# Attention and two MoE layers on one core: the first four attention tiles from plain query rows, with whole-tile exponentials

## The chip, the cores and the metric

The kernel runs on 1 core of one Trainium2 chip. The metric is the time of one execution in device microseconds (us); the time of a version is the median of several runs.

## What is computed

Chunked attention, then a leaky-ReLU layer pair, then a Mish layer pair, all in fp32 accuracy (the weights arrive as fp64 words and are converted on the chip).

```python
# attention: q, k, v of 4 batches x 8 heads x 768 positions x 64, 8 memory rows per head; chunk of 32 queries
for c in range(nc):                       # 24 chunks; left context 16, right context 8
    k_full = concat(mem_k, k[l_start:r_end])
    scores = scale * q_c @ k_full.T       # scale = 1/8
    scores = scores - max(scores)
    a = exp(scores)
    a = a / (sum(a) + 1e-09)
    out[c] = a @ concat(mem_v, v[l_start:r_end])
x = out as 3072 rows x 512
h = x @ w_in;  g = max(h, 0) + alpha * min(h, 0);  x = g @ w_out      # 512 -> 2048 -> 512
h = x @ w2_in; g = h * tanh(softplus(h));          y = g @ w2_out     # 512 -> 2048 -> 512
```

## The kernel before

The 3072 tokens are cut into 24 attention tiles T of 128 tokens and into 6 blocks of 512 tokens; block 0 takes the tiles T = 0 to 3 (`T0` = 4). For a block, `gemm1` (L1210) multiplies the block with a 128-column slice j of W_in (j = 0 to 15), `act1` (L1229, L1230 on ScalarE, L1233 on VectorE) applies the leaky ReLU, `split_g` (L1222, L1223) splits the result into a high and a low fp32r part, and `gemm2` (L1259) adds it into four PSUM banks. Each fp32 product is three fp32r products (high x high, high x low, low x high).

No engine order is written by hand. `Plan` collects tasks with an engine, a cost and a due time, and `Plan.run` schedules them: an engine takes the ready task with the earliest due time, and the due times come from the TensorE program, which is a list in order. The order of the instructions of each engine is then fixed. While TensorE would stand idle in the plan before the first `gemm2`, `Plan.run` fills in matmuls of a zero tile (`busy`, L1758).

The opening, up to the first `gemm1`, is this. For T = 0 to 3, `load_qk` loads the keys (`kw`, L626) and the query rows (L635), and `place` copies the rows (L277, on VectorE, for T = 0 also on ScalarE) into a tile `qbd` in which the two heads of a pair stand block-diagonal, with zeros written by GpSimd (L584). `scores_of` then computes 16 products of 128 x 64 x 64 per tile (L738) into a bank. `rest` of `scores_of` does the softmax: the row maximum (`top`, L753), for T = 0 and 1 a scaling of the maximum (L783) and eight exponentials of 64 columns each with their row sums (`exps`, L756, ScalarE); for T = 2 and 3 (`WHOLE`) one subtraction on VectorE (`less`, L763), one exponential of the whole tile (L766) and one row sum (`total`, L769); then 1e-9 is added (L786), the reciprocal taken (L787) and the tile multiplied (`norm`, L772). `turn_pe` transposes in two halves (L974), and `copy_on` (L277) takes each to the tile `aT`; `values_of` multiplies with the values (L805) and writes x as a high part (L822, ScalarE) and a low part (L826, VectorE). The scores lie in `s_bufs` and the transposes in `a_bufs`, two tiles of each, so T = 2 and 3 reuse the tiles of T = 0 and 1. The steps run in the order

```python
first = "s0 s1 t0 s2 t1 s3 v0 t2 v1 t3 v2 v3"
```

The weights come in through `load_raw` (L340 for W_in, L345 for W_out, 512 KB each), and `to_f32` turns the fp64 words into fp32: `scale` (L365, ScalarE), `high` (L368) and `low` (L371) on VectorE for the first eight; `split_w` makes the fp32r parts (L404 ScalarE, L407 VectorE). All loads stand in one queue, SP's. A `gate` (L608) is a DMA of one element out of a loaded tile: SP waits there until that tile has landed (or been scaled), and what stands behind it in the queue is issued only then. The first two columns of W_in are multiplied in two halves of the block's tokens, so that tokens of T = 0 and 1 don't wait for T = 2 and 3:

```python
for half in range(2):
    for j in range(SPLIT):          # SPLIT = 2
        gemm1(0, 0, j, xts[0], BN, half)
```

From T = 4 on other functions do the attention (`load_qk_late` L651, L658, L666; `scores_late` L861; `turn_late` L998; `values_late` L927), in pairs of tiles between the products of the blocks. They load into `kt` and into the same `qbd` tiles.

Of the kernel before, what the change touches and what calls it, by code (L numbers as in the profile page):

```python
# [200 lines left out]
def chunked_attention_moe_moe_kernel(  # L201
# [39 lines left out]
    WHOLE = (2, 3)  # L241
# [77 lines left out]
    PLAIN = 8  # L319
# [11 lines left out]

    def load_raw(item, **kw_):
        layer, side, j = item
        w = {(0, "i"): w1_in, (0, "o"): w1_out, (1, "i"): w2_in, (1, "o"): w2_out}[layer, side]
# [17 lines left out]
    def to_f32(item, raw, **kw_):  # L352
        late = bool(behind_wide)
        f = wfs.next()

        def words():
            t = raw.t if item[0] == 0 else raw.t.bitcast(U32).rearrange("p (f w) -> p f w", w=2)
            return t[:, :, 0], t[:, :, 1]
# [8 lines left out]
        def high():  # L367
            nc.vector.tensor_scalar(f.t, words()[1], 3, None, ALU.logical_shift_left)  # L368

        def low():  # L370
            nc.vector.scalar_tensor_tensor(f.t, words()[0], 29, f.t, ALU.logical_shift_right, ALU.bitwise_or)  # L371

        def three():
            t = raw.t.bitcast(U16)
            t = t if item[0] == 0 else t.rearrange("p (f w) -> p f w", w=4)
            nc.scalar.activation(words()[0], t[:, :, 1], AF.Identity, bias=floors, scale=2.0**-13)
# [7 lines left out]
        def both():  # L384
            nc.vector.scalar_tensor_tensor(f.t, words()[1], 3, words()[0], ALU.logical_shift_left, ALU.bitwise_or)

        if late:
            add("act", a_(512), negative, [raw], [f], **kw_)
        add("act", a_(512), scale, writes=[raw], **kw_)
        if item in w1_items[:2]:  # L390
            gate(raw, 0.0, lambda: words()[1][0:1, 0:1].bitcast(F32))
        if item in w1_items[:PLAIN]:
            add("dve", d_(512, True), high, [raw], [f])
            add("dve", d_(512), low, [raw], [f])
        else:
            add("act", a_(512), three, writes=[raw], **kw_)
            if late:
                add("dve", d_(512), with_negative, [f], [raw])
            add("dve", d_(512), both, [raw], [f])
# [161 lines left out]
    qbd = [own([P, 1024], f"qbd{i}") for i in range(2)] + [spare_slot() for _ in range(2, T0)]  # L561
# [9 lines left out]
    s_bufs = [own([P, 1024], "s"), spare_slot()]  # L571
    a_bufs = [own([P, 1024], "aT"), spare_slot()]
# [4 lines left out]
    for b in s_bufs:  # L577
        for cols in (slice(0, CH), slice(CH + SW, P)):
            add("pool", 0.6, lambda b=b, cols=cols: nc.gpsimd.memset(wide_of(b)[:, :, cols], 0.0), writes=[b])
    for b in qbd:  # L580
        for h in range(2):
            add(
                "pool", 0.6,
                lambda b=b, h=h: nc.gpsimd.memset(  # L584
                    b.t.rearrange("p (g h x) -> p g h x", g=2 * NP, h=2)[(1 - h) * 64 : (2 - h) * 64, :, h], 0.0
                ),
                writes=[(b, 2 + h)],
            )
    stats = ring(ac, [P, 3, 2 * NP], F32, "st", 3)
# [5 lines left out]
    n_ps = [0]  # L595

    def att_bank(T, late):
        n_ps[0] += 1
        return bank((0, 1, 2, 4, 5, 6, 7)[n_ps[0] % 7] if T < T0 else late)

    gated = dp.tile([1, 16], F32, name="gated")
    n_gates = [0]

    def gate(b, when, first=None):
        n = n_gates[0]
        n_gates[0] += 1
        add(
            "sp", 0.001, lambda: nc.sync.dma_start(gated[:, n : n + 1], first() if first else b.t[0:1, 0:1]), [b],  # L608
            at=-1.0, not_before=when,
        )  # L610

    def load_qk(T):
# [5 lines left out]
        qt = qbd[T]  # L618
# [4 lines left out]
        def qview():  # L623
            return qt.t.rearrange("p (a e h x) -> p a e h x", a=NP, e=2, h=2)

        add("sp", dma_(P * NP * KC * 4), lambda: nc.sync.dma_start(kview(), kw[b, t]), writes=[kt])  # L626
        if T == 3:
            gate(kt, 12.7)

        row = q_rows[T // 2], T % 2  # L630

# [3 lines left out]
        add("sp", dma_(P * 2048), lambda: nc.sync.dma_start(rows(), q[b, t].rearrange("h d a e x -> (h d) (a e x)")), writes=[row])  # L635
        for h in range(2):

            def place(eng, h=h):
                half = slice(h * 64, (h + 1) * 64)
                copy_on(eng, qview()[half, :, :, h], rows()[half].rearrange("p (a e x) -> p a e x", a=NP, e=2))  # L640
# [35 lines left out]
    def load_v(T):  # L676
        b, t = divmod(T, TPB)
        if T < T0:
# [3 lines left out]
            add("sp", dma_(P * 3520), lambda: nc.sync.dma_start(view(), src), writes=[v])  # L682
            if T in (0, 2):
                gate(v, 14.7 if T == 0 else 0.0)
# [31 lines left out]
    def scores_of(T):  # L716

        t = T % TPB
        (kt, kview), (qt, qview) = kts[T], qs[T]
        bk = att_bank(T, 6)  # L720
        sb = s_bufs[T % 2 if T < T0 else 0]

# [23 lines left out]
        def clip():  # L746
            if t == 0:
                nc.vector.memset(ps()[0:64, 0:NP, 0:16], NEG)
# [1211 lines left out]
```

## Time and profile before

| | |
|---|---|
| median of 3 runs | 1034.07 us (1033.57 to 1034.28) |
| profiled execution | 1034.0 us, its span 1032.1 us |
| TensorE busy | 1020.7 us, 99% of the span |
| granted TensorE clock, mean | 0.998 |
| VectorE, ScalarE, GpSimd busy | 834.1, 641.8, 6.9 us |
| first `gemm1` product starts | 23.59 us |
| third column of W_in (j = 2) starts | 30.47 us |

The execution's own time is 1.9 us over its span. A busy TensorE is the union of modelled intervals, so busy does not mean that every slot is used. Times below count from the span's start.

### The profile page before, as it was taken

The page shows a single profiled execution, that of the slowest core. Times are in us where ns is not written, and L with a number is a line of the kernel's source. Part 1 is how long each engine was busy: PE and PEld are TensorE (multiplying, and loading weights), DVE is VectorE, ACT ScalarE, POOL GpSimd, SP SyncE. Part 2 cuts the span into 40 slices and gives each one's busy share as a digit, 9 for nine tenths or more (in the row PEclk, how much of TensorE's full clock was granted, in tenths as well). Part 3 has the DMA queues.
Part 4 walks back from the last instruction along what each step waited for, and adds up shares of the span by engine and source line. Part 5 has one row for each costly group of instructions (what it writes and reads, how often), then busy time and mean ns, then how long its engine had stood idle before and what let it go on. Part 6 is the DMA issues. An engine that isn't in the chain of part 4 may idle for free.

```text
span 1032.1 us, 19612 instructions
## 1 busy us (share of the span) xinstructions
PE 1020.7 (99%) x7195; PEld 842.1 (82%) x7197; DVE 834.1 (81%) x1481; ACT 641.8 (62%) x1401; POOL 6.9 (1%) x20
## 2 busy tenths in 40 slices
PE   8999999999999999999999999999999999999997
PEld 6888888888888788888888888888888888888886
DVE  7877688888878889999999969697578777578784
ACT  6899756656665655797977657564444744444630
POOL 2000000000000000000000000000000000000000
PEclk9999999999999999999999999999999999999999
DMA  8977785875687773734878899886778766668766
GB/s 254 318 249 241 245 286 168 258 252 177 223 265 268 243 243 123 255 113 165 296 243 292 296 319 322 306 259 193 227 233 261 218 194 193 192 193 262 209 193 146
DMA packets 133929, 242.35 MB, mean 235 GB/s; under 512 B 12874, under 2 KB 50250, under 8 KB 133834
## 3 DMA queue, kind: packets, MB, share of 16 engines
q1 hardware_dynamic: 131658, 240.05, 73.6%
q10 hardware_dynamic: 2176, 1.05, 0.5%
q8 instruction: 57, 0.93, 0.4%
q14 instruction: 38, 0.31, 0.1%
HBM read 182.33 MB, written 58.72 MB: 234 GB/s over the span
## 4 chain that ended last, share of the span: by engine, by line
PE 97%; DMA 1%; ACT 0%; SPq 0%; issue 0%; DVE 0%; ACTq 0%
PE bank L1522 29%; PE bank L1364 22%; PE bank L1259 17%; PE bank L1210 17%; PE bank L1701 7%; PE bank L927 2%; PE bank L861 1%; DMA wo<-in_w_out_dram 1%; PE bank L1494 1%; DMA wo<-in_kw_dram 1%; PE bank L1758 0%; PE bank L805 0%; PE bank L738 0%; PE bank L998 0%; SPq L635 0%
## 5 line engine op out<-in xcount | busy, mean ns | idle before, releaser
L1210 PE MATMUL bank<-xh,wi 128*128 128x512 f32 (+1 forms) x528 | 170.1, 385 | 0.9 <-ACT rstrip L1230 0.9
L1259 PE MATMUL bank<-gh,wo 128*128 128x512 f32 x512 | 170.3, 392 | 0.2 <-issue 0.2
L1210 PEld LDWEIGHTS bank<-xh,wi 128*128 128x128 f32 x528 | 98.2, 188 | 20.7 <-ACT rstrip L1230 1.1
L1259 PEld LDWEIGHTS bank<-gh,wo 128*128 128x128 f32 x512 | 96.0, 188 | 20.6
L1364 PE MATMUL bank<-wo,wo 128*128 128x512 f32 x438 | 111.1, 389 | 0.0
L1210 PE MATMUL bank<-xl,wi 128*128 128x512 f32 (+1 forms) x264 | 101.1, 383 | 0.0
L1259 PE MATMUL bank<-gl,wo 128*128 128x512 f32 x256 | 99.7, 390 | 0.0
L1364 PEld LDWEIGHTS bank<-wo,wo 128*128 128x128 f32 x438 | 82.2, 188 | 17.0
L1522 PE MATMUL bank<-wi,wo 128*128 128x512 f32 x294 | 73.6, 389 | 0.0
L1229 ACT ACTIVATE rstrip<-bank 128x512 f32<-128x512 f32 x64 | 40.7, 636 | 50.7 <-PE bank L1210 50.4
L1364 PE MATMUL bank<-wo,wi 128*128 128x512 f32 x282 | 71.2, 389 | 0.0
L1522 PEld LDWEIGHTS bank<-wi,wo 128*128 128x128 f32 x294 | 55.2, 188 | 11.4
L1522 PE MATMUL bank<-wi,wi 128*128 128x512 f32 x258 | 64.5, 389 | 0.0
L1222 ACT CAST gh<-rstrip 128x512 fp32r<-128x512 f32 x64 | 42.5, 663 | 35.4 <-PE bank L1259 20.4
L1233 DVE SCALAR_TENSOR_TENSOR rstrip<-rstrip,nalpha 128x512 f32<-128x512 f32 x64 | 47.9, 749 | 19.6 <-ACT rstrip L1230 19.1
L1364 PEld LDWEIGHTS bank<-wo,wi 128*128 128x128 f32 x282 | 52.9, 188 | 11.0
L1223 DVE TENSOR_TENSOR gl<-rstrip,gh 128x512 fp32r<-128x512 f32 x64 | 44.2, 690 | 19.6 <-ACT gh L1222 18.8
L1522 PE MATMUL bank<-gh,wo 128*128 128x512 f32 x228 | 58.0, 389 | 0.0
L1015 DVE STREAM_TRANSPOSE aT<-s 32x256 f32<-32x256 f32 x128 | 55.7, 435 | 2.5
L1210 PEld LDWEIGHTS bank<-xl,wi 128*128 128x128 f32 x264 | 49.6, 188 | 9.4
L1522 PEld LDWEIGHTS bank<-wi,wi 128*128 128x128 f32 x258 | 48.4, 188 | 10.0
L1259 PEld LDWEIGHTS bank<-gl,wo 128*128 128x128 f32 x256 | 48.1, 188 | 10.1 <-issue 0.5
(354 smaller groups left out, 2181.7 us busy)
## 6 DMA issues: line engine op xcount, KB each, us to landing
wo<-w2i SPq DMA_DIRECT2D x102, 256.0 KB, 3.0
wo<-w2o SPq DMA_DIRECT2D x100, 256.0 KB, 3.7
wi<-w2o SPq DMA_DIRECT2D x68, 256.0 KB, 3.3
wi<-w2i SPq DMA_DIRECT2D x66, 256.0 KB, 3.1
wo<-in_w_out_dram SPq DMA_DIRECT2D x24, 512.0 KB, 6.8
w2i<-wo SPq DMA_DIRECT2D x24, 512.0 KB, 3.2
w2o<-wo SPq DMA_DIRECT2D x24, 512.0 KB, 3.2
wo<-w1o SPq DMA_DIRECT2D x22, 512.0 KB, 4.8
```

Of the source, the lines that this page charges most:

```text
L861: nc.tensor.matmul(ps(z)[row : row + CH, i, 2 * a + e, :], qview()[half, 2 * a + z, e].rearrange("p (x c) -> p x c", c=2)[:, :, c], keys(2 ...
L927: nc.tensor.matmul(out[h * 64 : (h + 1) * 64, i, p, c], value(half, c, 2 * p + h), aT()[half, i, (p % 2) * (NP // 2) + p // 2, c, h ^ (p % ...
L1015: nc.vector.transpose(dst[:, :, m // 2, m % 2], src[:, :, keys])
L1210: nc.tensor.matmul(bk.t[:, lo:hi], a, b, start=kk == 0 and i == 0, stop=kk == KT - 1 and i == 2)
L1222: add("act", a_(n), lambda: nc.scalar.copy(g.t[0], src.t[0]), [src], [(g, "h")], at=at)
L1223: add("dve", d_(n), lambda: nc.vector.tensor_sub(g.t[1], src.t[0], g.t[0].bitcast(F32)), [src, (g, "h")], [(g, "l")], at=at)
L1229: add("act", a_(n) - 0.05, lambda: nc.scalar.activation(m.t[0], h.t[:, :n], AF.Relu, scale=-1.0), [h], [m], at=at)
L1233: lambda: nc.vector.scalar_tensor_tensor(r.t[0], m.t[0], nalpha[:, j : j + 1], r.t[0], ALU.mult, ALU.add),
L1259: nc.tensor.matmul(bk.t[:, :n], lt, rh, start=j == 0 and i == 0, stop=j == NJ - 1 and i == 2)
L1364: nc.tensor.matmul(bk.t, l, r, start=start and kk == n == 0, stop=kk == 1 and n == 2, skip_group_check=True,)
L1522: nc.tensor.matmul(bs[db].t, l, r, start=first and k == 0, stop=p == pairs[-1] and k == 2, skip_group_check=True,)
L1701: nc.tensor.matmul(bk.t, l, r, start=start and kk == n == 0, stop=kk == 1 and n == 2, skip_group_check=True,)
```

## The change

Only the opening changes.

- Scores: the block-diagonal copies and their zeros go. The query rows are the stationary operand directly, 32 products of 64 x 32 x 64 per tile (two heads times two 32-query chunks, in different halves of rows and columns of the array).
- Softmax: all four tiles take whole-tile exponentials. For T = 0 and 1 VectorE subtracts the maximum (`less_here`); for T = 2 and 3 (`ON_PE`) TensorE adds the negated maximum to the scores' bank by one fp32 product of the identity with the broadcast maxima (`less`), and ScalarE reads the bank. The 1e-9 is now in two padding columns of the score tile, written once by GpSimd, and the row sum takes them in.
- Rooms: each of the four tiles has its own score tile (two of them the `qbd` tiles) and its own `aT` tile; banks are set by a table (`EARLY`).
- Order: the four scores first, then `t0 t1 v0 v1 t2 t3 v2 v3`.
- Loads: no gates; the first loads have fixed places in the queue; the first two columns of W_in come in one load of 1 MB (`load_first`), into the `xh1` tile, which block 1 uses later.

```diff
-    WHOLE = (2, 3)
+    ON_PE = (2,3,)
+    FIRST, PLAIN = 0, 8
+    def load_first():
+        raw = Buf(xmakers[1][0])
+        xring.last[1] = [raw]
+
+        def go():
+            to = raw.t.bitcast(U32).rearrange("p (k f) -> p k f", k=KT)
+            nc.sync.dma_start(to, w1_in[:, : 2 * P].bitcast(U32).rearrange("(k p) f -> p k f", p=P))
+
+        first_load(P * 8192, go, raw)
+        first_raw.append(raw)
...
+        if first_raw and item in w1_items[:2]:
+            return first_raw[0]
...
-        if item in w1_items[:2]:
-            gate(raw, 0.0, lambda: words()[1][0:1, 0:1].bitcast(F32))
...
-    qbd = [own([P, 1024], f"qbd{i}") for i in range(2)] + [spare_slot() for _ in range(2, T0)]
+    qbd = [own([P, 1024], f"qbd{i}") for i in range(2)]
...
-    s_bufs = [own([P, 1024], "s"), spare_slot()]
-    a_bufs = [own([P, 1024], "aT"), spare_slot()]
+    s_bufs = [own([P, 1024], "s"), spare_slot(), *qbd]
+    a_bufs = [own([P, 1024], "aT"), *(spare_slot() for _ in range(1, T0))]
...
+        for rows, col in ((slice(0, 64), CH - 1), (slice(64, P), CH + SW)):
+            add("pool", 0.1, lambda b=b, r=rows, c=col: nc.gpsimd.memset(wide_of(b)[r, :, c : c + 1], 1e-9), writes=[b])
...
+    EARLY = {"s": ((4,), (5,), (0,), (1,)), "t": ((6, 7), (2, 4), (7, 0), (1, 2)), "v": ((5,), (6,), (7,), (0,))}
...
+    def first_load(size, go, buf):
+        n_first[0] += 1
+        add("sp", size / 330e3, go, writes=[buf], at=n_first[0] - 100.0)
...
-            add(BOTH if T == 0 else "dve", 0.55, place if T == 0 else partial(place, "dve"), [row], [(qt, h)])
-        kts[T], qs[T] = (kt, kview), (qt, qview)
+        first_load(P * 2048, lambda: nc.sync.dma_start(rows(), q[b, t].rearrange("h d a e x -> (h d) (a e x)")), row)
+        first_load(P * NP * KC * 4, lambda: nc.sync.dma_start(kview(), kw[b, t]), kt)
+        kts[T], qs[T] = (kt, kview), (row, qview)
...
-                        nc.tensor.matmul(
-                            ps()[c * 64 : (c + 1) * 64, e * NP + p, :],
-                            qview()[:, p, e].rearrange("p h (x c) -> p (h x) c", c=2)[:, :, c],
-                            kview()[:, p, k0 : k0 + SW],
-                            start=True, stop=True,
-                        )
+                        for h in range(2):
+                            half, lo = slice(h * 64, (h + 1) * 64), c * 64 + h * CH
+                            nc.tensor.matmul(
+                                ps()[lo : lo + CH, e * NP + p, :],
+                                qview()[half, p, e].rearrange("p (x c) -> p x c", c=2)[:, :, c],
+                                kview()[half, p, k0 : k0 + SW],
+                                start=e == p == 0, stop=True, skip_group_check=True,
+                            )
...
         def less():
+            nc.tensor.matmul(
+                bk.t, ident, st.t[:, 0, :].unsqueeze(2).broadcast_to([P, 2 * NP, SW]), start=False, stop=True,
+                skip_group_check=True,
+            )
+
+        def less_here():
             nc.vector.tensor_add(s(), ps(), st.t[:, 0, :].unsqueeze(2).broadcast_to([P, 2 * NP, SW]))
 
         def exp():
-            nc.scalar.activation(s(), s(), AF.Exp, scale=0.125)
+            nc.scalar.activation(s(), ps() if T in ON_PE else s(), AF.Exp, scale=0.125)
...
-            if T in WHOLE:
-                add("dve", d_(512), less, [(st, 0), bk], [sb])
-                add("act", a_(512), exp, [], [sb])
-                add("dve", d_(512), total, [sb], [(st, 1)])
+            if T in ON_PE:
+                add("pe", 0.95, less, [(st, 0)], [bk])
             else:
-                add("dve", 0.12, lambda: nc.vector.tensor_scalar_mul(st.t[:, 0, :], st.t[:, 0, :], 0.125), [], [(st, 0)])
-                for g in range(2 * NP):
-                    add("act", 0.29, lambda g=g: exps(g), [(st, 0), bk], [(sb, g), (st, 1, g)])
-            add("dve", 0.12, lambda: nc.vector.tensor_scalar_add(st.t[:, 2, :], st.t[:, 1, :], 1e-9), [(st, 1)], [(st, 2)])
-            add("dve", 0.14, lambda: nc.vector.reciprocal(st.t[:, 2, :], st.t[:, 2, :]), [], [(st, 2)])
-            add("dve", d_(512), norm, [(st, 2)], [sb])
+                add("dve", d_(512), less_here, [(st, 0), bk], [sb])
+            add("act", a_(512), exp, [bk] if T in ON_PE else [], [sb])
+            add("dve", d_(512), total, [sb], [(st, 1)])
+            add("dve", 0.14, lambda: nc.vector.reciprocal(st.t[:, 2, :], st.t[:, 1, :]), [(st, 1)], [(st, 2)])
+            add("dve", d_(512), lambda: norm(nc.vector), [(st, 2)], [sb])
...
-    first = "s0 s1 t0 s2 t1 s3 v0 t2 v1 t3 v2 v3"
+    first = "s0 s1 s2 s3 t0 t1 v0 v1 t2 t3 v2 v3"
...
-    for T in range(T0):
-        load_v(T)
-    for st in block_steps[0]:
+    for go in (partial(load_v, 0), load_first, partial(load_v, 1), partial(load_v, 2), partial(load_v, 3)):
+        go()
```

How the order moves, in the names of the two programs (their line numbers are those of each program; numbers behind a name count buffers).

TensorE, from the scores of T = 3 to the values of T = 1, before: the transposes of T = 0 (`s`) and T = 1 (`wo_115`) follow, then the values of T = 0, with `busy` products in between.

```order
L738 MATMUL bank_237<-wo_178,wi_167 64x64 x16
L974 MATMUL bank_259<-ident,s 96x64 x8
L974 MATMUL bank_270<-ident,s 96x64 x8
L974 MATMUL bank_281<-ident,wo_115 96x64 x8
L974 MATMUL bank_295<-ident,wo_115 96x64 x8
L805 MATMUL bank_306<-aT,vw_207 64x64 x16
L1758 LDWEIGHTS busy
L1758 MATMUL bank_92<-busy 128x512
L805 MATMUL bank_332<-wi_304,wi_223 64x64 x16
```

After:

```order
L739 MATMUL bank_256<-wo_199,wi_121 32x64 x32
L754 MATMUL bank_211<-st_250,ident 128x512
L968 MATMUL bank_294<-ident,s 96x64 x8
L754 MATMUL bank_256<-st_291,ident 128x512
L968 MATMUL bank_311<-ident,s 96x64 x8
L968 MATMUL bank_325<-ident,wo_95 96x64 x8
L968 MATMUL bank_335<-ident,wo_95 96x64 x8
L968 MATMUL bank_347<-ident,qbd_107 96x64 x8
L799 MATMUL bank_360<-aT,vw_208 64x64 x16
L799 MATMUL bank_385<-wi_345,wi_306 64x64 x16
```

The two subtractions (L754, for T = 2 and 3) have come in behind the last scores, the first half of T = 2's transposes has moved ahead of the values of T = 0, and no `busy` product is left behind the scores.

VectorE, from the row sum of T = 2 to the last copy that the values of T = 2 wait for, after the change (`qbd_107` and `qbd_110` are the score tiles of T = 2 and 3, `wo_378` is the `aT` tile of T = 2):

```order
L766 TENSOR_REDUCE st_250<-qbd_107 128x8
L781 RECIPROCAL st_250<-st_250 128x8
L769 TENSOR_TENSOR qbd_107<-qbd_107,st_250 128x8x64
L766 TENSOR_REDUCE st_291<-qbd_110 128x8
L276 COPY wi_345<-bank_335 96x16x32
L781 RECIPROCAL st_291<-st_291 128x8
L769 TENSOR_TENSOR qbd_110<-qbd_110,st_291 128x8x64
L397 TENSOR_SCALAR wf<-xh_246 128x512
L400 SCALAR_TENSOR_TENSOR wf<-xh_246,wf 128x512
L397 TENSOR_SCALAR wf<-xh_246 128x512
L820 TENSOR_TENSOR xl_405<-bank_360,xh_404 128x4x128
L276 COPY wo_378<-bank_409 96x16x32
```

Before, two subtractions stand in this stretch, and the conversion of W_in (L368) comes behind both `norm`:

```order
L763 TENSOR_TENSOR s<-bank_190,st_219 128x8x64
L763 TENSOR_TENSOR wo_115<-bank_237,st_268 128x8x64
L277 COPY wi_304<-bank_295 96x16x32
L769 TENSOR_REDUCE st_219<-s 128x8
L769 TENSOR_REDUCE st_268<-wo_115 128x8
```

One copy of a transposed half has moved behind the conversion, to a place ahead of which four VectorE instructions of W_in and x now stand.

SP's queue, from the last keys of block 0 to the third column of W_in, before:

```order
L626 DMA wo_178<-in_kw_dram 128x672
L682 DMA vw_207<-in_vw_dram 96x2x512
L682 DMA wi_223<-in_vw_dram 96x2x512
L340 DMA wi_254<-in_w_in_dram 128x4x256
L608 DMA gated<-wo_178 1x1
L340 DMA wi_291<-in_w_in_dram 128x4x256
L608 DMA gated<-vw_207 1x1
L682 DMA wi_328<-in_vw_dram 96x2x512
L608 DMA gated<-wi_254 1x1
L682 DMA wi_358<-in_vw_dram 96x2x512
L608 DMA gated<-wi_291 1x1
L340 DMA wi_382<-in_w_in_dram 128x4x256
```

After:

```order
L643 DMA wo_199<-in_kw_dram 128x672
L683 DMA vw_208<-in_vw_dram 96x2x512
L340 DMA xh_246<-in_w_in_dram 128x4x512
L683 DMA wi_306<-in_vw_dram 96x2x512
L683 DMA wi_322<-in_vw_dram 96x2x512
L683 DMA wi_356<-in_vw_dram 96x2x512
L1755 DMA nalpha<-in_alpha_dram 128x16
L355 DMA wi_402<-in_w_in_dram 128x4x256
L360 DMA wo_441<-in_w_out_dram 128x1024
L355 DMA wi_487<-in_w_in_dram 128x4x256
```

The five gates are gone from the queue (the fifth, on the third value tile, stood behind this stretch), the two loads of W_in are one in second place, and alpha has moved from the sixth place to behind the values.

## Rows read from the trace of the kernel before

**Rows 1.** The page, part 1: busy time, share, instructions of each engine

```profile
PE 1020.7 (99%) x7195; PEld 842.1 (82%) x7197; DVE 834.1 (81%) x1481; ACT 641.8 (62%) x1401; POOL 6.9 (1%) x20
```

**Rows 2.** Stretches: length; busy of PE, PEld, DVE, ACT, POOL; clock, DMA, GB/s

```profile
5.00:10.00 5.00, 3.53 (x70) 2.36 (x65) 3.29 (x8) 1.32 (x9) 2.73 (x6) 1.00 1.03 353
...
40.00:60.00 20.00, 20.00 (x94) 16.56 (x94) 14.05 (x27) 19.65 (x60) 0.00 (x0) 1.00 0.99 265
60.00:100.00 40.00, 40.00 (x421) 33.02 (x420) 30.76 (x54) 40.00 (x98) 0.00 (x0) 1.00 0.75 242
```

**Rows 3.** Chain of waits, 0 to 60 us: start, length, what

```profile
20.89 5.95 DMA wo<-in_w_out_dram
...
28.81 0.62 ACT wo L404
...
30.47 3.02 PE bank L1210 x12
...
36.21 1.50 PE bank L861 x96
```

**Rows 4.** Timeline of TensorE, opening: start, length, line, what [idle before, releaser]

```profile
7.75 1.18 PE L738 MATMUL bank<-wo,qbd 128*64 128x64 f32 x32 [1.31 <-DVE qbd L277]
...
13.00 1.19 PE L738 MATMUL bank<-wo,wi 128*64 128x64 f32 x32
14.12 0.86 PE L974 MATMUL bank<-ident,s 64*96 64x64 f32 x15
...
14.90 0.82 PE L974 MATMUL bank<-ident,wo 64*96 64x64 f32 x15
...
21.54 1.15 PE L805 MATMUL bank<-aT,wi 96*64 96x64 f32 x32 [0.40 <-ACT aT L277]
22.52 1.14 PE L805 MATMUL bank<-wi,wi 96*64 96x64 f32 x32
23.59 0.39 PE L1210 MATMUL bank<-xh,wi 128*128 128x256 f32 x1
...
30.47 0.50 PE L1210 MATMUL bank<-xh,wi 128*128 128x512 f32 x1 [0.86 <-ACT rstrip L1230]
```

**Rows 5.** Timeline of SP's queue, opening

```profile
11.30 0.29 SPq L608 DMA_DIRECT2D gated<-wo  x1
...
20.06 0.38 SPq L340 DMA_DIRECT2D wi<-in_w_in_dram  x1
```

**Rows 6.** DMA, 0 to 40 us: GB/s of each microsecond

```profile
GB/s 0 27 297 352 282 342 324 363 399 338 241 241 247 266 336 349 194 66 33 166 225 164 362 374 307 340 350 394 354 384 373 398 396 364 375 372 372 382 375 369
```

**Rows 7.** Timeline of VectorE, opening

```profile
15.20 0.68 DVE L763 TENSOR_TENSOR s<-bank,st 128x512 f32<-128x512 f32 x1
15.79 0.68 DVE L763 TENSOR_TENSOR wo<-bank,st 128x512 f32<-128x512 f32 x1
...
18.37 0.33 DVE L787 RECIPROCAL st<-st 128x8 f32<-128x8 f32 x2
...
19.82 0.42 DVE L368 TENSOR_SCALAR wf<-wi 128x512 uint32<-128x512 uint32 x1
```

**Rows 8.** Timeline of ScalarE, opening and block 0

```profile
8.68 0.31 ACT L756 ACTIVATE s<-bank,st 128x64 f32<-128x64 f32 x1 [4.68 <-DVE st L783]
...
16.25 0.64 ACT L766 ACTIVATE s<-s 128x512 f32<-128x512 f32 x1
...
40.35 0.63 ACT L404 CAST wi<-wf 128x512 fp32r<-128x512 f32 x1 [2.07 <-DVE wf L371]
```

**Rows 9.** Timeline of TensorE, block 0: transposes of 128 columns, then j = 6

```profile
54.10 1.03 PE L998 MATMUL bank<-ident,s 128*128 128x128 f32 x8
54.89 0.48 PE L1210 MATMUL bank<-xh,wi 128*128 128x512 f32 x1
```

**Rows 10.** Timeline of VectorE, block 0: the low part of W_in column 6

```profile
53.47 0.69 DVE L407 TENSOR_TENSOR wi<-wf,wi 128x512 fp32r<-128x512 f32 x1
```

**Rows 11.** Chain of waits, 320 to 345 us

```profile
335.22 1.14 issue
```

More of the change, by code (lines that the diff above doesn't have):

```diff
@@ L578, in chunked_attention_moe_moe_kernel @@
         for cols in (slice(0, CH), slice(CH + SW, P)):
[L579 to L587, printed above, removed]
-            )
-    stats = ring(ac, [P, 3, 2 * NP], F32, "st", 3)
+            add("pool", 0.31, lambda b=b, cols=cols: nc.gpsimd.memset(wide_of(b)[:, :, cols], 0.0), writes=[b])
+        for rows, col in ((slice(0, 64), CH - 1), (slice(64, P), CH + SW)):
+            add("pool", 0.1, lambda b=b, r=rows, c=col: nc.gpsimd.memset(wide_of(b)[r, :, c : c + 1], 1e-9), writes=[b])
+    stats = ring(ac, [P, 3, 2 * NP], F32, "st", T0)
     stats2 = ring(ac, [P, 3, 4 * NP], F32, "su", 2)
@@ L594, in chunked_attention_moe_moe_kernel, with att_bank @@
     att_bufs = [*s_bufs[:1], *a_bufs[:1], *qbd[:2], *q_own, *upper]
[L595 to L610, printed above, removed]
+    EARLY = {"s": ((4,), (5,), (0,), (1,)), "t": ((6, 7), (2, 4), (7, 0), (1, 2)), "v": ((5,), (6,), (7,), (0,))}
+    def att_bank(T, kind, n=0):
+        return bank(EARLY[kind][T][n])
+    n_first = [0]
+    def first_load(size, go, buf):
+        n_first[0] += 1
+        add("sp", size / 330e3, go, writes=[buf], at=n_first[0] - 100.0)
     def load_qk(T):
@@ L617, in load_qk, with qview @@
         kt = kv_spare[T][0] if T in kv_spare else kring.next()
-        qt = qbd[T]
+        row = q_rows[T // 2], T % 2
         def kview():
             return kt.t[:, : NP * KC].rearrange("p (a c) -> p a c", a=NP)
[L623 to L630, printed above, removed]
         def rows():
             return row[0].t[:, row[1] * 512 : (row[1] + 1) * 512]
[L635 to L640, printed above, removed]
-            add(BOTH if T == 0 else "dve", 0.55, place if T == 0 else partial(place, "dve"), [row], [(qt, h)])
-        kts[T], qs[T] = (kt, kview), (qt, qview)
+        def qview():
+            return rows().rearrange("p (a e x) -> p a e x", a=NP, e=2)
+        first_load(P * 2048, lambda: nc.sync.dma_start(rows(), q[b, t].rearrange("h d a e x -> (h d) (a e x)")), row)
+        first_load(P * NP * KC * 4, lambda: nc.sync.dma_start(kview(), kw[b, t]), kt)
+        kts[T], qs[T] = (kt, kview), (row, qview)
         att_bufs.append(kt)
@@ L960, in turn_pe @@
         sb = ss.pop(T)
[L961 removed]
+        ab = a_bufs[T]
         def aT():
@@ L1793, in chunked_attention_moe_moe_kernel, with first_products @@
     sent_ = [0]
-    for half in range(2):
+    def first_products(half):
         for j in range(SPLIT):
             gemm1(0, 0, j, xts[0], BN, half)
+    first_products(0)
+    for st in block_steps[0][FIRST_HALF:]:
+        run_step(st)
+    first_products(1)
     for layer, blk, j in tiles:
```

85 lines of the change are left out of this document (43 added, 42 removed).

## The prediction

> **What bounds the kernel now.** I read the busy times first. TensorE is busy 1020.7 of 1032.1 us, no other engine comes near [rows 1]. Then the stretches: from 40 to 100 us TensorE is busy all the time, at granted clock 1.00, which is its upper level of 2.4 GHz [rows 2]. So an instruction saved on another engine is worth nothing there, and the change touches nothing there or later. Next the chain of waits of the first 60 us: from 30.47 us, where the third column of W_in (j = 2) begins, it is TensorE alone; ahead of that it passes through a load and ScalarE [rows 3]. So the time changes by as much as the start of j = 2 moves, unless block 0 cannot follow. That start is set by two things. The first products begin at 23.59 us, behind the values of T = 3, and j = 2 then waits 0.86 us for ScalarE [rows 4]. The wait comes from afar: j = 2 writes the bank of j = 0, whose reads by ScalarE stand behind the cast of W_out 0 at 28.81, which needs a load that was issued at 20.89 and landed 5.95 us later, at 26.84 [rows 3]. It was issued so late because SP sat at gates: the load of W_in 2 ahead of it went out at 20.06 [rows 5], after the queues had fallen to 66 and 33 GB/s in the microseconds 17 and 18 [rows 6].
>
> **The loads without gates.** The sizes follow from the shapes in the order (KB of 1024 bytes): query rows 256, keys 336, values 384, the double W_in load 1024, each other weight 512. Queries and keys are 4 x 592 = 2368 KB = 2.42 MB. The rates [rows 6] add up to 2.39 MB at 9.0 us, so their last byte moves at about 9.1; the gate on those keys opened at 11.30 [rows 5]. I take 2.2 us from last byte to signal. The same sums give 4.40 MB at 16.0 us; beyond that I use 350 GB/s, about the mean of the microseconds 22 to 25 (346). In the new order the double W_in load (3.87 MB in) lands at 14.4 + 2.2 = 16.6 us, the values of T = 1 (4.26 MB) at 17.8, those of T = 3 (5.05 MB) at 20.1, W_in 2 (5.57 MB) at 21.5 and W_out 0 (6.09 MB) at 23.0, which is 3.8 us earlier than before.
>
> **Scores.** The copies into the block-diagonal tiles go, and with them the 1.31 us that TensorE waited for one at 7.75 [rows 4]. The scores then wait for keys only: T = 3 at 11.2 us (the gate's time), where before it began at 13.00 behind planned `busy` products. Thirty-two products of the new shape cost half of the 1.50 us that 64 such products take at 36.21 [rows 3], 0.75 us. If they didn't run side by side they would cost 32 x 0.07 = 2.24 us, at the 0.07 us of the 16 old products in 1.12 us from 13.00 to 14.12 [rows 4]. I take 0.75, because it is the same shape, and keep 2.24 for the range. VectorE can read T = 3's bank at about 12.15.
>
> **Softmax.** ScalarE loses the 16 exponentials of 64 columns that began at 8.68 and gets two more of a whole tile, 0.64 us each [rows 8]; it is then no longer on the path. VectorE loses two subtractions, two scalings and four additions of 1e-9, but gains two row sums and two subtractions for T = 0 and 1. The path now runs through VectorE. From the maximum of T = 3 to the copy of T = 2's second transposed half its order has ten full-size instructions, at 0.60 us start to start (15.20 to 15.79), two `high` of 0.42, and three reciprocals, 0.25 each with the wait for the result before them (0.33 for a pair) [rows 7]: 6.0 + 0.84 + 0.75 = 7.6 us, so 12.15 + 7.6 = 19.75.
>
> The subtraction on TensorE (`less`) has no row of its own. From below: eight fp32 transposes of 128 columns take 54.89 - 54.10 = 0.79 us [rows 9], so 0.40 us for 512 columns. From above: the old scores took 1.12 us for 16 products of 64 columns [rows 4], two of which can share the array, so at most 1.12 us for eight in a row. I take 0.85, nearer to the scores, which are products as `less` is. Both stand behind the scores of T = 3, at 12.0 and 13.2, each followed by 0.4 us of transposes (two halves start 0.78 apart, 14.12 to 14.90). ScalarE can then exponentiate T = 2 at 13.05 and T = 3 at 14.3, just ahead of VectorE's two row sums at 13.7 and 15.3. With 1.12 the path grows by 0.3, with 0.40 by nothing. The Trainium skill ("FP8 and Floating Point Precision", TensorE Precision Notes) says that true fp32 takes four passes through the array; four times the 0.227 us of an fp32r product would be 0.91 us (an estimate), and the sum would be the same.
>
> **First products.** The values of T = 2 start at 19.85, and two tiles of values take 0.98 + 1.07 us [rows 4]; their own loads are there (20.1 for T = 3). So the first products start at 22.0 instead of 23.59: 1.6 us. From there to j = 2 it was 6.88 us, 0.86 of it the wait [rows 4]. W_out 0 lands at 23.0, its cast can be done near 26.3, and ScalarE's reads of j = 0's bank, finished at 26.4, end near 27.6. So the wait goes and j = 2 starts at 22.0 + 6.0 = 28.0, **2.5 us earlier**. Next late would be those reads, 0.4 us behind.
>
> **At nothing I cost** the padding writes on GpSimd (they replace longer ones and are needed by the first row sum, past 8 us); alpha's later load (needed past 27); and the new wait of SP for the `qbd` tiles, which are now the score tiles of T = 2 and 3. Their next loads stand behind W_out 1, and W_in 4 and W_out 2 are queued behind them. T = 3's transposes end near 19.4, while 7.5 MB ahead of that place keep the queues busy until about 25 us. If the transposes came after that, SP would hold back W_in 4, and every microsecond would count only past the slack of j = 4, which starts 13 us after j = 2.
>
> **The sum.** 1034.0 us (the profiled execution, 0.07 under the median) - 1.6 - 0.9 = **1031.5 us**. A difference under 0.2% (2.1 us) can't be told from no change, so "faster" begins at 1032.0.
>
> **Rivals.**
> - *Block 0 can't follow* (chance 0.12). ScalarE is busy without a gap from 40 to 100 us [rows 2], and the low part of W_in 6 was done at 53.47 + 0.69 = 54.16, 0.73 us before its use at 54.89 [rows 9, 10]. If ScalarE's weights stayed where they are, TensorE could come only 0.7 us forward: 1033.3. Against it: ScalarE idled 2.07 us before 40.35 for a VectorE instruction [rows 8], which in the new order comes ahead of the late scores' work; and its loads come earlier.
> - *Half of it* (0.13). Loads land later than my sum, ScalarE again stands in order before one (W_in 2, W_out 0 or W_in 3), and the 0.86 us come back: 1034.0 - 1.6 = 1032.4. For it: five value and weight loads now share the queues with W_in 2.
> - *More* (0.14). Later orders shift too. A wait of 1.14 us for keys stands at 335.22 [rows 11]; if the new order loads them in time, 1031.5 - 1.1 = 1030.4.
> - *The clock falls* (0.05), the slower side. Of 28 `busy` products 17 stay, and none behind the scores of T = 3. From 11.2 to 22 us TensorE has some 9.8 us of work: scores 0.75, `less` 1.7, transposes 8 x 0.4, values 4 x 1.05. At half clock (1.2 GHz) that is 19.6 us, and the first products start at 31 instead of 23.59: 1034.0 + 7.2 = 1041. It decides as soon as the clock drops before the values of T = 0. Against it: in 5 to 10 us TensorE was busy 3.53 of 5.00 us and kept clock 1.00 [rows 2]; the new opening has no emptier stretch by my times. The Trainium skill ("TensorE: Matmul & The Clock Gate", Parts 1 and 4) says that the clock falls to half after idleness, and that transposes don't count as busy in the same way. By that rule the stretch without `busy` products is in danger; the row agrees with the lower danger, as far as it reaches, and no row here has a stretch of transposes without `busy` products.
>
> **Numbers.** My forecast has 0.56. Its own range is 1030.9 to 1032.4 (`less` +0.3, landings 0.5 either way, half of the scores' upper bound); about three quarters of it is under 1032.0. Faster: 0.43 + 0.14 and a part of "half" = 0.61. Slower: 0.05 for the clock and 0.01 for others. Same: 0.33. The range reaches from 1029.7 ("more", with early landings) to 1033.5 ("block 0 can't follow") and leaves out the clock and the tails.
>
> **What would show it.** Right: the first product near 22.0, j = 2 near 28.0 with no wait on ScalarE before it, W_out 0 landing near 23, VectorE without gaps from 12 to 20 us, and TensorE without gaps from there on. Wrong: scores of T = 3 that take 2 us; a granted clock under 1.00 before 25 us; ScalarE waiting for a weight load between 21 and 27 us; idle TensorE at j = 6 or at other places past 40 us.

## The result: slower, and the profile after

| | old kernel | changed kernel |
|---|---|---|
| median | 1034.25 us (1033.57 to 1037.43, 6 runs) | 1044.94 us (1040.90 to 1054.16, 6 runs) |
| ratio, 95% interval | | 1.0113 [1.0067, 1.016] |
| profiled execution, its span | 1034.0, 1032.1 us | 1051.14, 1049.3 us |
| granted clock, mean | 0.998 | 0.988 |
| first product, j = 2 | 23.59, 30.47 us | 33.98, 41.50 us |

The forecast of 1031.5 us and its range missed, on the other side of no change. The profiled execution is one of the long ones; the mean clock of the six goes with their time: 0.987 and 0.988 for 1054.16 and 1051.14 us, 0.997 for 1040.90 and 1042.97.

Page of the changed kernel, part 1, the line that answers to [rows 1]:

```profile
PE 1034.2 (99%) x7317; PEld 849.9 (81%) x7317; DVE 833.4 (79%) x1472; ACT 636.9 (61%) x1368; POOL 3.6 (0%) x24
```

TensorE is as busy as before. So the stretches come next (columns as in [rows 2]):

```profile
10.00:15.00 5.00, 1.90 (x55) 0.94 (x44) 2.46 (x5) 0.63 (x1) 0.00 (x0) 0.89 1.05 280
15.00:20.00 5.00, 5.00 (x63) 3.18 (x63) 2.06 (x4) 0.85 (x2) 0.00 (x0) 0.50 1.07 233
20.00:25.00 5.00, 5.00 (x44) 3.35 (x45) 3.02 (x7) 3.02 (x6) 0.26 (x1) 0.50 1.08 327
25.00:30.00 5.00, 5.00 (x82) 4.88 (x79) 3.10 (x7) 2.41 (x5) 0.00 (x0) 0.50 0.44 149
30.00:40.00 10.00, 10.00 (x105) 9.74 (x104) 8.00 (x14) 5.67 (x10) 0.00 (x0) 0.61 0.92 289
40.00:60.00 20.00, 20.00 (x216) 16.74 (x216) 15.62 (x28) 17.31 (x43) 0.00 (x0) 1.00 1.05 281
```

From 15 us on TensorE is busy in every microsecond, but at clock 0.50, the lower level of 1.2 GHz; it is back at 1.00 only behind the first dense products. Ahead of that stands a stretch with 1.90 us of work in 5.00. Its timeline, TensorE (to compare with [rows 4]):

```profile
11.74 0.42 PE L739 MATMUL bank<-wo,wi 64*32 64x64 f32 x12 [0.27 <-DMA wo<-in_kw_dram]
14.99 1.71 PE L739 MATMUL bank<-wo,wi 64*32 64x64 f32 x52 [2.83 <-issue]
16.62 2.07 PE L754 MATMUL bank<-st,ident 128*128 128x512 f32 x2
...
24.43 1.97 PE L799 MATMUL bank<-aT,vw 96*64 96x64 f32 x32
...
33.98 0.58 PE L1204 MATMUL bank<-xh,wi 128*128 128x256 f32 x1
```

The scores of T = 3 are 64 records in one task (an fp32 product leaves two). After 12 of them TensorE stops for 2.83 us, and the trace names nothing that it waits for. What moved on the DMA queues from 12 to 13 us (queue and kind: packets, MB, share of the 16 engines):

```profile
q1 hardware_dynamic: 132, 0.27, 95.4%
q8 instruction: 1, 0.02, 7.6%
```

In this microsecond a packet of instructions went through, beside loads that fill the queues. The page counts 58 such packets and 0.95 MB on q8 over the whole run, 16 KB each. That fits TensorE's program: 7317 matmul records with as many weight loads are 14634 instructions, 252 for each packet. TensorE goes on 2.7 us behind this packet's start, and in the openings of the runs below each stop inside a task with no named cause ends 2.4 to 2.8 us behind one.

To see where the delay arises I compared the start of the n-th product of 512 columns in both TensorE timelines: the changed kernel is 11.0 us behind at j = 2 and still 10.8 at 280 us, so block 0 follows without loss or gain. Behind that it loses more: 12.7 at 383 us, 15.5 at 473, 16.2 at 501, 17.0 at the end. That stretch wasn't edited. But `Plan.run` ordered it anew: past 200 us the order of every engine differs, with five copies on another engine. The four longest of eight kinds of TensorE wait past 200 us in the changed kernel (us in total, times, longest):

```profile
PE bank L1253 <- DMA wo<-w1o: 1.2, 1, 1.2
PE bank L1253 <- issue: 0.7, 1, 0.7
PE bank L1253 <- ACT rstrip L276: 0.6, 1, 0.6
PE bank L1695 <- ACT b L1702: 0.5, 1, 0.5
```

### The profile page after: what moved, and what is told of

The parts are those of the page before. It is cut to its first block, busy times and chain, and to the rows that moved or that the text cites. A ratio compares the mean times of both kernels' runs of the same rounds, so it can differ in the third digit from the quotient of the medians.

```text
span 1049.3 us, 19778 instructions
## 1 busy us (share of the span) xinstructions
PE 1034.2 (99%) x7317; PEld 849.9 (81%) x7317; DVE 833.4 (79%) x1472; ACT 636.9 (61%) x1368; POOL 3.6 (0%) x24
## 4 chain that ended last, share of the span: by engine, by line
PE 88%; DVE 6%; DMA 3%; issue 1%; ACT 1%; SPq 0%; DVEq 0%; ACTq 0%
PE bank L1516 28%; PE bank L1358 22%; PE bank L1204 16%; PE bank L1253 15%; PE bank L921 2%; PE bank L1695 2%; PE bank L855 1%; DVE wo L489 1%; DMA wo<-in_kw_dram 1%; PE bank L799 1%; DMA raw<-in_w_out_dram 1%; PE bank L968 1%; DMA raw<-in_w_in_dram 1%; DVE b L1666 1%; PE bank L1488 1%
```

## The experiments

Four theories at first. **A**: TensorE's next block of instructions is a DMA and comes late because nothing gates the loads any more; that is the stop in the scores of T = 3, and the clock falls behind it. **B**: the clock falls for want of `busy` products behind the scores. **C**: the late loss comes from the other order past 200 us. **D**: it comes from the late opening itself. Each kernel below ran beside the old one; ratios are to that, with 95% intervals.

**a1, one gate.** SP waits for the keys of T = 3 before the double W_in load; all orders stay.

```diff
+            nc.sync.dma_start(gated[:, 0:1], kts[3][0].t[0:1, 0:1])
             nc.sync.dma_start(to, w1_in[:, : 2 * P]...)
```

> The changed kernel, but SP waits for the keys of T = 3 before it issues the double load of W_in and all behind it; every engine's order else as changed. Theory A (TensorE's own instructions come by DMA; between 12.15 and 14.99 us it stood 2.83 us inside the scores of T = 3 with nothing to wait for, while an instruction packet was under way on full DMA engines, and the clock fell then): the wait inside the scores of T = 3 falls under 0.7 us, the clock stays 1.00, the first W_in product starts at 22 to 24 us instead of 34; the time is 1036 to 1041 us, with the stalls past 200 us left. Theory B (the clock falls because no products of the zero tile stand behind the scores): the wait may go, the clock still falls to 0.5 between 12 and 25 us, first product past 30 us, 1042 us or more.

Measured: 1041.25 us, 1.0068 [1.0045, 1.0091], clock 0.998 or 0.999 in all four executions. Its TensorE timeline:

```profile
12.50 0.42 PE L741 MATMUL bank<-wo,wi 64*32 64x64 f32 x12
13.54 0.97 PE L741 MATMUL bank<-wo,wi 64*32 64x64 f32 x52 [0.62 <-issue]
...
18.70 1.15 PE L801 MATMUL bank<-aT,vw 96*64 96x64 f32 x30
20.73 0.33 PE L801 MATMUL bank<-aT,vw 96*64 96x64 f32 x2 [0.89 <-issue]
...
25.56 0.39 PE L1206 MATMUL bank<-xh,wi 128*128 128x256 f32 x1
```

The same stop, behind the same 12th record, but 0.62 us instead of 2.83; then a second one, 126 records later (52 + 44 with `less` and transposes + 30), and in the first products a third of 1.24 us. The clock holds. j = 2 is 2.3 us behind the old kernel instead of 11.0, a little under the 2.75 us of the three waits. Past 280 us it loses 4 us more (+2.4 there, +6.8 at the end): the gate does nothing to that. A's wait and clock came as expected; the first product (25.56 against 22 to 24) and the time came later. Not all of the shorter stop is the gate's: TensorE went on 1.45 us sooner (13.54 against 14.99), but it also came to the 12th record 0.8 us later (12.92 against 12.16), since its scores of T = 0 began 0.6 us later and those of T = 1 took 1.73 us instead of 1.10.

**a2, more `busy` products.** 14 of them: 6 behind the scores of T = 3, 4 behind the transposes and 4 behind the values of T = 1.

```diff
+    MORE_BUSY = {("s", 3): 6, ("t", 1): 4, ("v", 1): 4}
```

> The changed kernel with 14 more products of the zero tile: 6 behind the scores of T = 3, 4 behind the transposes of T = 1, 4 behind the values of T = 1, orders else unchanged. Theory A: the 2.8 us wait in the scores of T = 3 stays and the clock falls behind it as before, perhaps for a shorter time: first product past 29 us, time within 4 us of the changed kernel. Theory B: clock 1.00 or back by 18 us, first product at 25 to 28 us, 1037 to 1041 us.

Measured: 1048.41 us, 1.0139 [1.0109, 1.017]. The stop is 3.46 us here; the clock is 0.66 from 15 to 20 us and 1.00 from 20 to 60, so it is back some 19 us sooner than in the changed kernel, and the first product comes at 30.91 us, j = 2 6.3 us behind the old kernel. Past 280 us it loses 8 us more (+14.5 at the end). The stop stands ahead of all 14 products, so B isn't the cause. That the products brought the clock back isn't shown either: in e6 below it came back by 17.4 us with none of them behind the scores.

**a3 and b1, the order past 200 us.** The planned tasks past 200 us are the same 1:1 in both kernels; a table of their numbers gives one kernel the other's order (and engine for the five copies). a3: the changed opening with the old order. b1: the old opening with the new order.

```diff
-        for _, _, fn in sorted(extra, key=lambda x: x[:2]):
+        for _, _, fn in sorted(extra, key=lambda x: (x[1] in rank, rank.get(x[1], x[0]), x[1])):
```

> The changed kernel with the opening as changed, but all tasks that the plan starts past 200 us in the order of the kernel before (a table of task numbers). Theory C (the stalls of 7 us past 300 us come from the other order there): they fall to under 2 us in the profile, and the time is 5 to 7 us under the changed kernel at the same clock: 1034 to 1048, as the clock goes. Theory D (they come from the later opening itself): 5 us of stalls or more stay.

> The kernel before with its own opening, but all tasks past 200 us in the order of the changed kernel. Theory C: the stalls near 331, 346, 381, 440 to 500 and 652 us appear at places about 11 us earlier, 5 to 7 us in all; 1039 to 1041 us at clock 0.998. Theory D: as before, 1033 to 1036 us.

Measured: a3 1039.80 us, 1.0061 [1.0036, 1.0087]; b1 1041.59 us, 1.007 [1.0047, 1.0093]. All of TensorE's waits past 200 us in a3:

```profile
PE bank L1464 <- issue: 0.5, 1, 0.5
PE bank L1906 <- ACT b L1913: 0.2, 1, 0.2
```

In a3, which is 6.5 us late at 280 us, nothing more is lost (+6.2 at the end), so D falls. b1 is 1.4 us ahead of the old kernel's trace until 250 us and 6.8 behind at the end: 8 us lost in a stretch that starts on time. C holds. Its largest wait, TensorE at 371 us:

```profile
371.23 0.30 PE L1073 MATMUL bank<-qbd 64*32 64x64 f32 x4 [3.06 <-issue]
```

It lies inside the 128 score records of two tiles, and q8's packet moved at 368.8 us, 2.4 us ahead: the opening's stop once more. The old kernel has a stop at the same count (4154 records in, 4153 in b1), but of 0.18 us and three products behind such scores. From 366 to 370 us the DMA share was 0.84 there and 1.00 in b1.

**a4, both repairs.** Gate and old order.

> The changed opening with one gate (SP waits for the keys of T = 3 before the double W_in load) and, past 200 us, the old kernel's order. If the loss of 10.8 us has two independent parts, the opening (instruction blocks that come late on full queues, and the clock that falls behind that) and the order past 200 us, both are mostly taken away here: clock 0.99 or over, first products near 25.6 us and j = 2 near 32.7 us as with the gate alone (2.2 us behind the old kernel's 30.47), late stalls under 1.5 us in all, and a time of 1035 to 1037 us. If the late loss comes from the later opening itself and not from the order, the late stalls are 3 us or more and the time is near 1040 us. If both parts are one thing (a3 and a1 recover the same 4 to 5 us), it is near 1040 us as well.

Measured: 1037.75 us, 1.004 [1.0023, 1.0057], late waits 0.59 us. The parts nearly add up: from 1044.94, the gate alone takes 3.7 us off, the order alone 5.1, both 7.2. But the time is 0.75 us over its range, and the opening missed its expectation: in the profiled execution the first two stops were 1.38 and 1.98 us (0.62 and 0.89 in a1), and behind the second the clock fell to 0.50. The gate at that place makes the stops short, not sure to be short. The nine executions divide by the clock: five at a mean of 0.999 or 1.000 took 1035.0 to 1037.75 us, four at 0.988 to 0.994 took 1039.3 to 1041.6.

**a5, the gate further ahead**, before the values of T = 0; old order.

> As the run before, but the gate stands further ahead, before the values of T = 0, so that nothing but queries and keys is on the queues while the scores run. If TensorE stalls in the scores of T = 3 because its next block of instructions waits behind data on the queues, the block is moved before 10.5 us here, and the stall in the scores of T = 3 (0.62 us with the later gate, 2.5 to 3.5 us without one) falls under 0.4 us; the values and W_in come some 2 us later, so the next blocks fall in full queues again and the sum is the same or up to 2 us better: 1033 to 1036 us. If the stall has nothing to do with queues, it stays at 0.6 us or more at the same product, and the time is later by the later loads: 1036 to 1039 us.

Measured: 1038.48 us, 1.0043 [1.0029, 1.0057]. TensorE:

```profile
11.14 1.18 PE L956 MATMUL bank<-wo,wi 64*32 64x64 f32 x64
12.25 1.12 PE L971 MATMUL bank<-st,ident 128*128 128x512 f32 x2
...
16.51 1.15 PE L1016 MATMUL bank<-aT,vw 96*64 96x64 f32 x32
21.00 1.98 PE L1016 MATMUL bank<-wi,wi 96*64 96x64 f32 x32 [3.33 <-DMA wi<-in_vw_dram]
```

All 64 scores of T = 3 run through; the instruction packet moved in the microsecond from 8 to 9, where it was 12 to 13 in the changed kernel. The price is a later load: the values of T = 1 stand behind the double W_in load, TensorE waits 3.33 us for them, the clock falls all the same, and the time misses its 1033 to 1036 us.

The traces of all nine versions of this opening agree on the queues. Counted from TensorE's start on the last 126 records before the block's end, the packet moves 4.2 to 5.0 us later without a gate (the changed kernel, a2, a3), 2.6 to 2.9 with a1's gate (a1, a4, e6) and 1.3 to 1.9 with this one (a5, a6, a7). That it is asked for at that point is a reading; that it moves sooner where fewer loads stand ahead of it is what the three groups show.

**e6, does the stop go by count?** a1 without the `busy` products between the scores.

> The changed opening with the gate of a1, without the busy products that stand between the scores (those ahead of the first scores stay); the order past 200 us is the changed kernel's. A busy product is one instruction pair, and the stall in the scores of T = 3 came behind record 12 of 64 in every run of this opening. If it is a block of instructions that ends there, the stall moves back by as many records as busy products are left out, 7: it comes behind record 18 to 20. If it is something that T = 3 waits for (a part of its keys, its bank), it stays behind record 12. The time says little here, 1040 to 1050 us, since the clock may fall.

Measured (one execution, 1042.25 us), TensorE and its stretches:

```profile
11.41 0.54 PE L741 MATMUL bank<-wo,wi 64*32 64x64 f32 x22 [0.42 <-DMA wo<-in_kw_dram]
13.64 1.12 PE L741 MATMUL bank<-wo,wi 64*32 64x64 f32 x42 [1.70 <-issue]
```

```profile
10.00:15.00 5.00, 2.88 (x112) 2.41 (x104) 3.54 (x8) 0.63 (x1) 0.00 (x0) 0.90 0.63 170
15.00:20.00 5.00, 5.00 (x42) 2.66 (x42) 3.41 (x7) 2.40 (x5) 0.00 (x0) 0.76 1.07 298
20.00:25.00 5.00, 4.38 (x117) 4.12 (x116) 4.93 (x11) 4.76 (x10) 0.26 (x1) 1.00 1.07 322
```

The stop moved back by 10 records. The expectation said 7, read off a trace that lacks a few rows; the program has 2 + 4 + 4 = 10 products there. So 221 records lie ahead of the stop either way: 7 + 64 + 2 + 64 + 4 + 64 + 4 + 12 with them, 7 + 192 + 22 without. It isn't something that T = 3 waits for. The clock fell behind this stop too, but only for 3.4 us (at 0.90 and 0.76 of 5 us each, so 1.0 and 2.4 us at 0.50). It came back behind scores, one `less` and eight transposes, where the changed kernel stayed at 0.50 behind the same work.

**b2, b3, b4: the old kernel without gates, with every score product issued twice (the second writes the same result again), and both.** These take the changed kernel's two properties, free loads and 64 score records per tile, into the old opening.

```diff
-            "sp", 0.001, lambda: nc.sync.dma_start(gated[:, n : n + 1], ...), [b],
+            "sp", 0.001, lambda: None, [b],
...
-                        nc.tensor.matmul(
+                        for _ in range(2):
+                            nc.tensor.matmul(
```

> The old kernel without its gates; all else, the order of every engine too, is the old one. It tells what the full queues alone do to an opening with 32 score records per tile instead of 64. If late blocks of instructions on full queues are the cause, its TensorE meets a late block as well, at the values of T = 1, where a block ended before (0.25 us of wait at 17.33 us): 1 to 3 us of wait there, first products 24.5 to 27 us instead of 23.59, total 1034 to 1038 us, unless loads that come earlier give back more at j = 2. If queues don't matter and only the new scores and products do, its first products come at 23.6 us or earlier and the time is 1032 to 1034 us.

> The old kernel, gates and all, in which every score product of the first four tiles is issued twice (the second writes the same result over the first): 64 score records per tile, as in the changed kernel, on the old queues. TensorE has slack there, 4 times 0.6 us beside 2.5 us of busy products. If the number of TensorE instructions matters by the blocks in which they are loaded, the first block ends where the count reaches 221 records as in the changed kernel, which is 6 records into the scores of T = 3 (8 + 64 + 2 + 64 + 5 + 64 + 8 ahead of them); with the gates the block comes in time or nearly, a wait of 0 to 1 us, and the time is 1034 to 1036 us. If new scores cost by their shape or by the place of the other steps, nothing happens at record 6 and the time is 1034.

> The same without the gates. Neither part costs much alone by now (without gates: 1.0005 of the old time). If a late block needs both, many instructions and full queues, TensorE stops behind record 5 to 7 of the scores of T = 3 for 1.5 to 3 us, and once more some 125 records later; first products 25 to 28 us (later still if the clock falls behind the wait), total 1036 to 1041 us. If the loss of the changed opening lies in its new steps (the subtraction on TensorE, the order of scores and transposes) instead, this kernel stays within 1.5 us of the one without gates: 1034 to 1036 us.

| | median us | ratio, 95% interval | delay at j = 2 |
|---|---|---|---|
| b2, no gates | 1034.89 | 1.0005 [0.9995, 1.0015] | -0.7 us |
| b3, scores twice | 1037.91 | 1.0041 [1.0026, 1.0057] | +3.6 us |
| b4, both | 1041.69 | 1.0075 [1.0061, 1.0089] | +7.5 us |

b2 missed the first expectation's price: it meets a late block too (0.76 us, 345 records in, in the values of T = 3 and not of T = 1), but starts its first product at 23.91 us and loses no time that can be told from none. b3 has no stop, and still took 1.9 us more than its range; its cost is plain work that I had called slack (64 old-shape records take 2.2 us, and the scores of T = 3 start at 15.70 instead of 13.00). b4, TensorE:

```profile
15.46 0.45 PE L739 MATMUL bank<-wo,wi 128*64 128x64 f32 x5
16.09 2.02 PE L739 MATMUL bank<-wo,wi 128*64 128x64 f32 x59 [0.17 <-issue]
...
21.24 0.33 PE L806 MATMUL bank<-wi,wi 96*64 96x64 f32 x3 [0.25 <-issue]
23.74 1.86 PE L806 MATMUL bank<-wi,wi 96*64 96x64 f32 x29 [2.17 <-issue]
```

It breaks behind record 5 of T = 3, 215 + 5 = 220 records in, as forecast; the slow scores have given that block time, so only 0.17 us. The next break is 127 records on (59 + 32 + 32 + 1 + 3), a wait of 2.17 us, and then the clock falls, the first product comes at 32.13 us, and the time is 0.7 us over its range:

```profile
20.00:25.00 5.00, 2.57 (x59) 2.39 (x60) 5.00 (x13) 2.34 (x5) 0.00 (x0) 0.81 1.06 369
25.00:30.00 5.00, 5.00 (x48) 3.22 (x44) 1.91 (x4) 2.19 (x5) 0.00 (x0) 0.50 1.06 381
```

Free loads cost 0.6 us (interval -0.5 to 1.6) with 32 records per tile and 3.8 us (1041.69 - 1037.91) with 64. None of the new steps (`less`, the order of the scores, the rooms) is in b4.

**a6 and a7, the best of this opening.** a6 is a5 with the values of T = 1 issued ahead of the double W_in load. a7 moves also the conversions of the first two columns behind the copies of the transposes.

```diff
+        first = sorted(range(95, 105), key=lambda i: (start[i], i))
+        start = [max(t, 18.95 + 0.01 * first.index(i)) if i in first else t for i, t in enumerate(start)]
```

> The best version of the changed opening that the runs point to: the early gate, the values of T = 1 issued ahead of the double W_in load (in each other's place), and the old order past 200 us. The early gate took away the wait in the scores of T = 3, but TensorE then waited 3.33 us for the values of T = 1 and the clock fell. With them ahead of W_in this wait should fall under 0.5 us and the clock stay at 1.00 from 15 to 30 us; the W_in load lands near 20.5 us, first products near 24.5 to 25.5 us, j = 2 near 31 to 32 us (30.47 in the old kernel), total 1034.5 to 1036.5 us: the changed opening's own best, no better than the old one. If the clock falls all the same, 1037 to 1039 us.

> As a6 (early gate, values of T = 1 ahead of the double W_in load, old order past 200 us), with the conversions of the first two columns of W_in moved on ScalarE and VectorE behind the copies of the transposes of T = 2 and 3. In a6 these copies stood behind a conversion that waited for the W_in load (landed at 20.39 us), and TensorE waited 4.09 us for the copy. If that order is all that is left, the wait of 4.09 us goes, the values of T = 3 end near 22 us, and the first products wait for W_in alone: 20.4 us and five conversion steps of 0.43 to 0.69 us make 23.5 to 24.5 us, j = 2 at 30.5 to 31.5 us with clock 1.00 and a time of 1033.5 to 1035.5 us, the same as the old kernel. If the idle time before the first products (1.5 to 2.5 us) or a late block of instructions in them makes the clock fall, it is 1036 to 1039 us.

Measured: a6 1038.03 us, 1.0042 [1.003, 1.0055]; a7 1036.93 us, 1.0025 [1.0012, 1.0037]; both lie in the range given for a clock that falls all the same. In a6 the wait for the values is gone, and another is late next, on TensorE and (second fence) ScalarE:

```profile
23.97 1.98 PE L1020 MATMUL bank<-wo,wi 96*64 96x64 f32 x32 [4.09 <-DVE wo L487]
```

```profile
20.39 0.65 ACT L608 ACTIVATE xh<-xh 128x512 f32<-128x512 f32 x1 [3.71 <-DMA xh<-in_w_in_dram]
20.95 0.56 ACT L487 COPY wo<-bank 96x512 f32<-96x512 f32 x1
```

The copies of the transposes stand behind a conversion that waits for W_in. With that order changed (a7) this wait is gone, but the second block of instructions is late again:

```profile
16.20 1.15 PE L1022 MATMUL bank<-aT,vw 96*64 96x64 f32 x30
18.78 0.33 PE L1022 MATMUL bank<-aT,vw 96*64 96x64 f32 x2 [1.44 <-issue]
18.90 1.89 PE L1022 MATMUL bank<-wi,wi 96*64 96x64 f32 x32
```

and the clock is 0.50 from 20 to 30 us. No version of the new opening that ran beats the old kernel.

## Why the prediction was wrong, step by step

- **"The change touches nothing there or later"** failed. The edit is in the opening, but the planner ordered everything behind it anew, and the sum had this at nothing. That order costs half of the loss or more: the old order takes 5.1 of the 10.7 us off the changed kernel, and b1 is 8.0 us over the old one (1041.59 against 1033.63). "More" did say that later orders shift, but only as a gain. I had compared the two orders in the opening alone.
- **The loads without gates**: right in size for W_in (16.6 us forecast; issued at 5.44, 11.6 us to landing, so 17.0), 2.0 us short for W_out 0 (23.0 against 11.62 + 13.4 = 25.0). What failed is that the loads alone were counted. TensorE's instructions move over the same DMA engines, and the sum had a wait for them at nothing: it was 2.83 us, and the clock fell in it and stood at 0.50 until 37.8 us (0.89 of 10 to 15 us, 0.61 of 30 to 40).
- **Scores, 0.75 us per tile**: mis-sized. They take 1.03 us start to start at full clock (8.96 to 9.99 in a4), and T = 3 began at 11.74 instead of 11.2. Alone that is 0.8 us at T = 3. What mattered was the count: 64 records per tile where there were 32.
- **`less`, 0.85 us**: 1.06 at full clock (14.44 to 15.50 in a1), inside its bounds; twice 1.0 more at half clock.
- **The path through VectorE** didn't bind: VectorE waited 4.26 us for the scores of T = 3 before its maximum at 16.73.
- **First products at 22.0**: 33.98. By a1 against the changed kernel, 8.7 of the 11.0 us at j = 2 (11.0 - 2.3) go with the long stop and the clock behind it, in one execution of each; a1's own 2.3 us stand against 2.75 us of short stops.
- **The 0.86 us wait of j = 2**: over-read. In b1, with the same opening orders as before, j = 2 started 1.4 us earlier and without a wait. A gap of under 1 us in one execution of this opening was no base for a term of 0.9.
- **"The clock falls" (0.05)** is what happened, with its own condition met (0.50 from 15 us, ahead of the values of T = 0 at 24.43) and its price near: 31 and 1041 forecast, 33.98 and 1044.9 measured. I set it low by [rows 2], where 3.53 us of work in 5.00 kept the clock at 1.00, and by my own times, which had no emptier stretch. The stop made one: 1.90 in 5.00. So the fall came with a stop, not for the missing `busy` products that I had counted there. That the time came near is luck in part: it holds the late order too, and with the old late order the changed opening took 1039.80 us (a3). On the rule of the Trainium skill that I weighed there ("TensorE: Matmul & The Clock Gate", Parts 1 and 4): the fall behind idleness agrees with the runs. For the part on transposes, the same transposes ran at 1.00 in a1, so they alone don't bring a fall; in e6 the clock came back in a stretch with them, in the changed kernel it didn't, and whether they delay the return no run separates.
- **"Block 0 can't follow"** fell: 11.0 us late at j = 2 and 10.8 at 280 us. **"More"** rested on the wait of 1.14 us in [rows 11], which I took for keys; it is likely a block of instructions as well, since it lies 381 records, three times 127, ahead of the stop of 0.18 us that the old kernel has at 368 us. But the q8 packet moved 3.1 us before its end, earlier than at the other stops, so this isn't shown.

Left open: why the new order past 200 us loses what it does. The waits that the trace names past 200 us are 4.55 us in the changed kernel and 1.32 in the old one, about half of the 6.2 us lost there in the profiled execution; I didn't trace the rest, nor try which of the moved tasks does it. The subtraction on VectorE for T = 2 and 3 wasn't tried either.

## What to carry to other kernels

Count an engine's instructions, not only their time: a shape that halves the time of a product and doubles the number of them uses up its program faster, and the program arrives over the DMA engines that the loads fill. A gate that looks like lost bandwidth may be what lets it through; before gates go, look where TensorE stops inside a task with no releaser named, and whether an instruction packet moved some 2.5 us ahead. Where a planner sets the order, compare the whole order of the two kernels and pin what the edit doesn't mean to move: here that was worth as much as the edit.

## What the runs showed of the hardware

- TensorE's program comes in blocks: stops at 220 or 221 records and 126 or 127 records on, in openings of different shape, and moved by the exact count when products are left out. A record comes with its weight load, so 126 records are 252 instructions. The Trainium skill ("Runtime: NRT & Kernel Launch", Instruction fetch mechanics) has blocks of 16 KiB or 256 instructions that the sequencer fetches by a DMA queue of its own while the present block runs, and calls the cost mostly hidden. The size agrees with the runs (58 packets, 0.95 MB). Hidden it is not, where small products meet full queues: up to 3.46 us a block in the openings (a2), 3.06 us in b1 at 371 us.
- The clock fell to 0.50 in or just behind waits of 1.44 us (a7), 1.70 (e6), 1.98 (a4), 2.17 (b4), 2.83 (the changed kernel), 3.06 (b1), 3.33 (a5), 3.46 (a2) and 4.09 (a6). It held behind a1's 0.62, 0.89 and 1.24, but also behind a first wait of 2.54 us in a3, where it fell only after a second of 1.71. So the length of a wait alone doesn't decide it.
